# Four moves in a hand-written order: a turn, a fold, a square root and a difference of weights

## The chip, the core and the metric

The kernel runs on one core of a Trainium2 chip. A core has five engines that run side by side, each with its own queue of instructions that is worked off strictly in order: TensorE (PE: matmuls, with its weight loads shown as PEld), VectorE (DVE), ScalarE (ACT), GpSimd (POOL) and SyncE (SP), which here only issues DMAs. Engines wait for one another through semaphores. An instruction that waits holds up everything queued behind it on its engine.

The metric is the device time of one execution in microseconds, as the median of several runs. Times inside an execution come from one profiled execution and are counted from the start of its span.

## What is computed

The input is four batches of 768 tokens, eight heads of 40 features. The first half is an mLSTM cell; the second a Fourier mix with a two-layer network:

```python
for t in range(S):
    m_new = np.maximum(f_gate[:, :, t] + m, i_gate[:, :, t])
    f_stab = np.exp(f_gate[:, :, t] + m - m_new)
    i_stab = np.exp(i_gate[:, :, t] - m_new)
    m = m_new
    C = f_stab * C + i_stab * einsum('bhd,bhe->bhde', vt, kt)
    n = f_stab * n + i_stab * kt
    h_tilde = einsum('bhde,bhe->bhd', C, qt)
    denom = np.maximum(np.abs(nq), 1.0)          # nq = n . q
    y[:, :, t] = sigmoid(o_gate) * h_tilde / denom
x = y as (B, S, H*D)                              # 4 x 768 x 320
u = x + np.real(fft(fft(x, axis=1), axis=2))
un = (u - mean(u)) / np.sqrt(var(u) + 1e-06)      # over the 320 features
out = u + np.maximum(un @ w_ch1, 0.0) @ w_ch2     # 320 -> 1280 -> 320
```

(Indices of the broadcasts are left out.)

## The kernel before

**Stages.** Each batch goes through three stages. The *mLSTM* works on six chunks of 128 tokens; a chunk has scores (L465), an exponential (L421, ACT), a mask (L443, POOL), a weighing (L471, DVE), a product with the state `ph` (L479) and with the chunk (L486), a product into the new state `pc` (L496), a gather (L511 to L529), a *turn*, which is four transposes into a tile `px` (L535, PE), and a *finish*, which divides by the denominator and writes x (L544 to L550, five DVE instructions). The *mix* folds pairs of chunks, (2,3), then (1,4), then (0,5), into even and odd parts (`mix_fold`: L606, L609, L613, L618, L613 on DVE, for pair (2,3) three more on POOL). It multiplies them with tables of cosines and sines, adds the result to x and gets the mean and variance of each row. For batches 2 and 3 `mix_fold_again` folds the folds once more in three steps (POOL L635; DVE L638 with POOL L639 to L642; DVE L644 with POOL L645). The *MLP* of a batch takes 32 slots.

**The order is written by hand.** `at(slot, phase, function, ...)` puts a function into a plan, and `run` calls all of them sorted by slot and, within a slot, by phase: EVAC is 0, FILL 1, MAIN 2, FILL_PE 3, with fractions between. The order of these calls is the order in every engine's queue. MAIN holds the MLP's matmuls, one piece to a slot; everything else is put around them. Batch 0's MLP runs in slots 31 to 62, batch 1's in 63 to 94, batch 2's in 95 to 126, batch 3's in 127 to 158. The mLSTM of batch 1 begins at slot 32 (chunk c at 32 + 3c), of batch 2 at 50, of batch 3 at 82, so each runs beside the MLP of the batch before.

**The sets.** From batch 1 on, the first layer's 10 blocks of 128 hidden features are done as five *sets* of four slots each (`mlp_block`, steps 0 to 3), in a form with seven products in place of eight for two blocks and two groups of tokens. It adds results with DVE: step 1 has one addition (L906, `h12 += p5`), step 2 three (`h12 += p3`, `h22 += p5`, `h11 += p2`), just behind the two tails (L902, matmuls of the remaining 64 features, which add into p3, p5, p2 and p1). Four PSUM banks are used in turn, and in the other direction in every second set. Step 3 begins the next set (L897, in `begin`) in the bank that p3 held, which the first of the three additions frees. A tail into p5 also has to wait for step 1's addition, which reads p5. Set i of batch b occupies the slots s_mlp + 4i to s_mlp + 4i + 3 and i counts from 0, so the third set of batch 1 has its step 1 in slot 72 and its step 2 in 73.

**The second layer** (`mlp_out_pair`, L1016) is in a similar form, for which DVE forms differences of w_ch2 once (`out_weight_sums`, L988, four of them, the last in place). `mix_rstd` computes 1/sqrt(var + 1e-6) for a batch: four DVE operations on 128x6 (L785 to L790), then twelve on POOL (L792 to L795). Its result is first used in the residuals of the second layer (L966).

**The turned chunks' buffers.** `ps_h` is a PSUM pool of two buffers, taken in turn by `ph`, `pc` and, for batches 1 to 3, `px`, in the order of the calls. A new tile waits until the tile before it in the same buffer has been read for the last time: `ph` by the gather's copies on ACT (L517, L519, L524, L528), `pc` by the gather's additions on DVE (L515), `px` by the finish. In batch 1, chunk 2 is turned in slot 45 and finished in 46, chunk 3 turned in 46 and finished in 47, chunk 4 gets its `ph` and `pc` in 47 and is turned in 49, and chunk 5 gets its `ph` in 50.

**Weight pieces.** The weights arrive as float64 and are converted in pieces by DVE and ACT (`take` L344 and L346, `convert` L351 and L352, `join` L358, L360 and L364). The last piece is taken in slot 45 and joined in slot 47.

`plan_mlstm`, `plan_mix` and `plan_batch` fill the plan with these slots. The list that `plan_batch` calls `done` is the slots of the three folds (`x_done` in `plan_mix`): for batch 1 they are 48, 51 and 54.

Of the kernel before, what the change touches and what calls it, by code (L numbers as in the profile page):

```python
# [20 lines left out]
NT = S // L  # L21
# [5 lines left out]
NFF = DFF // L  # L27
TAIL = DM - 2 * L
TG = NT // 2
# [21 lines left out]
def kernel(  # L51
# [70 lines left out]
    def at(slot, phase, fn, *args):  # L122
        plan.setdefault((slot, phase), []).append((fn, args))
# [7 lines left out]
    EVAC, FILL, MAIN, FILL_PE = range(4)  # L131
# [421 lines left out]
    def plan_mlstm(b, s0, stride=3):  # L553
        for c in range(NT):
            s = s0 + stride * c
            if b > 0:
                t = 22 + 2 * c if b == 1 and c < 3 else s - 5
                at(t, FILL, mlstm_load, b, c)
                at(t, FILL, mlstm_load_max, b, c)
                at(t, FILL, mlstm_load_decay, b, c)  # L560
                at(s, FILL, mlstm_load_o, b, c)
            if (b, c) > (0, 0):
                at(s, FILL, mlstm_exp, b, c, 0)
                at(s + 1, FILL - 0.5, mlstm_exp, b, c, NP)
                last = (b, c) == (0, NT - 1)
                at(s - 1 if last else s, FILL_PE + (2.05 if last else 2), mlstm_scores, b, c)
                if b > 0:
                    at(s + 1, FILL, mlstm_mask, b, c)
            at(s, FILL, mlstm_scale_v, b, c)
            at(s if (b, c) == (0, 2) else s + 1, FILL + 0.1, mlstm_scale_q, b, c)  # L570
            at(s + 2, FILL, mlstm_decay, b, c)
            end = (b, c) == (0, NT - 1)
            at(s + 1 if end else s + 2, FILL - 0.4 if end else FILL, mlstm_weigh, b, c)
            at(s + 2 if end else s + 3, FILL_PE, mlstm_from_state, b, c)
            at(s + 2 if end else s + 3, FILL_PE + (2 if end else 3), mlstm_from_chunk, b, c)
            at(s + 3, FILL_PE + 3, mlstm_to_state, b, c)
            at(s + 3 if end else s + 4, FILL, mlstm_gather, b, c)
            if b == 0:
                t, x = ((8, 11), (11, 14), (13, 14), (14, 15.5), (17, 18), (18, 21))[c]
            else:  # L580
                t = s + (8, 8, 7, 5, 5, 5)[c]
                x = t + 1
            at(t, FILL_PE + ((2.5 if c < 4 else 1) if b == 0 else 1), mlstm_turn, b, c, b == 0 and c < 4)
            at(x, FILL + 0.05, mlstm_finish, b, c)
# [212 lines left out]
    def plan_mix(b, s0, x_done, s_feat, s_add, s_turn):  # L797
        for j in range(TG):
            p = TG - 1 - j
            at(x_done[j], FILL + 0.5 if b < 2 else FILL_PE + 0.2, mix_fold, b, p)  # L800
            if b == 0:
                at((s0 - 4, s0 - 2, s0)[j], FILL_PE + 4, mix_seq, b, p, (0, 1))
                at((s0 - 2, s0 - 2, s0)[j], FILL_PE + 4, mix_tail, b, p)
            elif b == 1 or j == 0:
                if b > 1:
                    for step, slot in enumerate((x_done[0], x_done[-1] + 2, x_done[-1] + 6)):
                        at(slot, FILL_PE + 0.25, mix_fold_again, b, step)
                at(s0, FILL_PE + 4, mix_seq, b, p, (0,))
                at(s0 + 1, FILL_PE + 4, mix_seq, b, p, (1,))
                at(s0 + 2, FILL_PE + 4, mix_tail, b, p)  # L810
        for i in range(2):
            at(s0 + 1 if b == 0 else s0 + 1 + i, FILL, mix_seq_out, b, i)
        at(s0 + (1 if b == 0 else 3), FILL + 0.1, mix_tail_out, b)
        for p in range(TG):
            at(s_feat[p], FILL_PE + 4, mix_feat, b, p)
        for c, a, t in zip(ORDER, s_add, s_turn):
            at(a, FILL if b < 2 else MAIN + 0.5, mix_add, b, c)
            at(t, FILL + 0.1, mix_center, b, c)
            at(t, FILL_PE + (5 if b == 0 or c in ORDER[:4] else -0.1), mix_turn, b, c)
            if b > 0:  # L820
                at(t, FILL_PE + 6, mix_turn_out, b, c)
            elif t < s_mlp:
                at(t + 1, FILL + 0.2, mix_turn_out, b, c)
            else:
                at(t + 1, EVAC, mix_turn_out, b, c)
# [221 lines left out]
    def plan_mlp(b, s):  # L1047
        groups = range(NT // TG)
        for i in range(NFF // 2) if b > 0 else ():
            for step in range(4):  # L1050
                at(s, MAIN, mlp_block, b, i, step)
                s += 1
            end = i == NFF // 2 - 1
            for n, (gr, f) in enumerate(((1, 2 * i + 1), (1, 2 * i), (0, 2 * i))):
                at(*((s - 1, MAIN + (-0.1 if gr else 0.1)) if end else (s + n, MAIN + 0.5)), mlp_relu_in_place, gr, f)
        for gr in groups if b == 0 else ():
            for f in range(NFF):
                at(s, MAIN, mlp_in, b, gr, f)
                s += 1
                if f % 2:  # L1060
                    at(s, EVAC, mlp_relu, b, gr, f - 1)
                    at(s, EVAC, mlp_relu, b, gr, f)
        if b > 0:
            for j in range(1, 5):
                at(s - (5, 4, 3, 3)[j - 1], FILL_PE + 0.3, hidden_sums, 0, (j,), 0, NFF // 2 - 2)
            at(s, EVAC, hidden_sums, 0, (1, 2), NFF // 2 - 2, NFF // 2)
            at(s, MAIN + 0.1, hidden_sums, 0, (3, 4), NFF // 2 - 2, NFF // 2)
        for n in range(TG) if b > 0 else ():
            for step in range(4):
                at(s, MAIN, mlp_out_pair, b, n, step)  # L1070
                if n < TG - 1 and step > 1:
                    for j in (2 * step - 3, 2 * step - 2):
                        at(s, MAIN + 0.6, hidden_sums, n + 1, (j,))
                s += 1
        for gr in groups if b == 0 else ():
            for i in range(TG):
                for half in range(2):
                    at(s, MAIN, mlp_out, b, gr, i, half)
                    s += 1
                at(s, EVAC, mlp_store, b, gr, i)  # L1080
# [5 lines left out]

    def plan_batch(b, s_mlstm, s_mix, s_mlp):
        plan_mlstm(b, s_mlstm)
        done = [s_mlstm + 3 * (j + NT // 2) + 7 for j in range(NT // 2)]
        assert s_mix >= done[-1] and s_mlp >= s_mix + 9  # L1090
        late = [s_mlp + 2 * c for c in range(TG)]
        if b == 0:
            feat = [s_mix + 1, s_mix + 1, s_mlp + 3]
            turn = [s_mix + 2, s_mix + 3, s_mix + 4]
            add = turn + [s_mlp, s_mlp + 4, s_mlp + 6]
            late = [s_mlp + 2, s_mlp + 5, s_mlp + 7]
        else:
            feat = [s_mix + c for c in ((3, 4, 6) if b == 1 else (3, 4, 7))]
            add = [s_mix + c for c in ((4, 4, 5, 6, 7, 7) if b == 1 else (4, 4, 5, 6, 8, 9))]
            turn = [s_mix + c for c in ((5, 6, 6) if b == 1 else (6, 7, 8))]  # L1100
            late = [s_mix + c for c in ((7, 8, 8) if b == 1 else (9, 10, 10))]
            at(s_mlp, EVAC + 0.5, mlp_sums)
        plan_mix(b, s_mix, done, feat, add, turn + late)
        at(s_mlp + NFF, FILL + 0.6, mix_rstd, b)
        plan_mlp(b, s_mlp)

    s_mlp = 31
    plan_batch(0, 0, 22, s_mlp)
    plan_batch(1, 32, 54, s_mlp + MLP_SLOTS)
    plan_batch(2, 50, 83, s_mlp + 2 * MLP_SLOTS)  # L1110
    plan_batch(3, 82, 115, s_mlp + 3 * MLP_SLOTS)
    for n in range(4):
        at(s_mlp + 2 * NFF + 1 + n, FILL + 0.4, weight_sums, n)
        at((56, 57, 58, 72)[n], FILL + 0.4, out_weight_sums, n)

    at(60, FILL + 0.4, lambda: nc.gpsimd.memset(ds_sb[0:1, 0, 0, :], 1.0))

# [131 lines left out]
```

## Time and profile before

| | us |
|---|---|
| median of 5 runs | 422.54 |
| the five runs | 422.41, 422.47, 422.54, 423.66, 423.70 |
| the profiled execution's own time | 423.66 |
| its span in the profile | 421.9 |

| engine | busy us | share of the span | instructions |
|---|---|---|---|
| PE | 408.0 | 97% | 2966 |
| PE weight loads | 304.6 | 72% | 2966 |
| DVE | 288.5 | 68% | 682 |
| ACT | 189.0 | 45% | 493 |
| POOL | 112.9 | 27% | 194 |

The span is the time from the first to the last instruction in the profile; the execution's own time has 1.76 us more around it. A busy share is an average over the whole span. Matmuls are pipelined and their ends are modelled, so the busy time of PE says that work is in it, not that it runs at its peak. The granted TensorE clock was 1.00 throughout. The chain of work that ended last consists of PE for 74% of the span, DVE 11%, DMA 8%, issue 3%, ACT 2% and POOL 2%; the DMA pieces of it all lie before 110 us.

### The profile page before, as it was taken

The numbers are of one execution on the slowest core, as the hardware profiler recorded it, in microseconds if no ns is written. First come the engines' busy times: TensorE is split into PE (matmuls) and PEld (weight loads), VectorE is DVE, ScalarE is ACT, GpSimd is POOL, SyncE is SP. The second block draws the span as 40 slices with busy tenths as digits, with TensorE's granted clock in tenths as the row PEclk, the third lists the DMA queues.
The fourth block names the chain that finished last, engine by engine and source line by source line (L and its number), as shares of the span: only waits on it lengthen the run. The fifth ranks groups of instructions, "written<-read, shape, count | busy, mean of one in ns | idle before, by whom it ended". The sixth has DMA issues, their size and how long they took to land.

```text
span 421.9 us, 8013 instructions
## 1 busy us (share of the span) xinstructions
PE 408.0 (97%) x2966; PEld 304.6 (72%) x2966; DVE 288.5 (68%) x682; ACT 189.0 (45%) x493; POOL 112.9 (27%) x194
## 2 busy tenths in 40 slices
PE   8999999999899999999899999999999999999997
PEld 6877554576567678777458899977559989555996
DVE  7789893867895729686855488796844686335552
ACT  6986375677452321664357413554452023355000
POOL 5654201459340720433041341333130000020000
PEclk9999999999999999999999999999999999999999
DMA  7799297457765353364300344310000000000010
GB/s 230 251 270 312 81 274 261 141 181 222 234 161 167 102 154 99 103 207 138 109 0 2 128 125 144 121 54 2 0 2 0 33 31 18 16 2 0 16 48 31
DMA packets 20549, 47.14 MB, mean 112 GB/s; under 512 B 2784, under 2 KB 9312, under 8 KB 20384
## 3 DMA queue, kind: packets, MB, share of 16 engines
q1 hardware_dynamic: 20512, 46.65, 36.3%
q8 instruction: 23, 0.38, 0.4%
q14 instruction: 14, 0.11, 0.1%
HBM read 42.52 MB, written 4.11 MB: 111 GB/s over the span
## 4 chain that ended last, share of the span: by engine, by line
PE 74%; DVE 11%; DMA 8%; issue 3%; ACT 2%; POOL 2%; DVEq 0%; ACTq 0%; POOLq 0%; SPq 0%
PE po L1016 18%; PE pm L897 15%; PE po L960 8%; PE ps L465 5%; PE pm L902 4%; PE ph L486 4%; DMA kvt<-in_kv 4%; PE ph L479 3%; DMA raw<-in_w 3%; PE pu L729 3%; PE px L535 2%; DMA qk<-in_qkT 2%; PE pz L698 2%; PE put L772 1%; PE pM L218 1%
## 5 line engine op out<-in xcount | busy, mean ns | idle before, releaser
L966 DVE SCALAR_TENSOR_TENSOR x<-po,rstd,x 128x160 f32<-128x160 f32 (+1 forms) x69 | 27.0, 395 | 41.4 <-PE po L1016 35.5
L906 DVE TENSOR_TENSOR h<-h,pm 128x384 f32<-128x384 f32 x60 | 30.5, 550 | 31.3 <-PE pm L897 16.0
L421 ACT ACTIVATE W<-W,colT 128x128 f32<-128x128 f32 x144 | 45.0, 395 | 0.0
L443 POOL TENSOR_SCALAR_AFFINE_SELECT W<-W 128x1024 f32<-128x1024 f32 x18 | 21.3, 1184 | 80.2 <-ACT W L421 58.5
L897 PE MATMUL pm<-uT,w_sb 128*128 128x384 f32 x90 | 37.5, 503 | 1.9 <-DVE h L906 1.6
L960 PE MATMUL po<-w_sb,h 128*128 128x320 f32 x120 | 34.4, 435 | 0.0
L471 DVE TENSOR_TENSOR W<-ps,W 128x512 f32<-128x512 f32 x48 | 30.7, 681 | 4.2 <-POOL W L443 4.0
L837 PE MATMUL pm<-uT,w_sb 128*128 128x384 f32 x80 | 29.9, 500 | 1.7 <-DMA qk<-in_qkT 1.0
L777 ACT COPY uT<-put 128x384 f32<-128x384 f32 x24 | 11.2, 478 | 40.2 <-PE put L772 40.2
L960 PEld LDWEIGHTS po<-w_sb,h 128*128 128x128 f32 x120 | 22.2, 190 | 9.5 <-issue 0.8
L1016 PE MATMUL po<-T,S 128*128 128x160 f32 x180 | 27.9, 302 | 0.3 <-DVE x L966 0.3
L465 PE MATMUL ps<-qk 40*128 40x128 f32 x384 | 27.8, 284 | 0.0
L1016 PEld LDWEIGHTS po<-T,S 128*128 128x128 f32 x180 | 25.5, 190 | 1.7 <-DVE x L966 0.5
L792 POOL TENSOR_TENSOR t<-rstd 128x6 f32<-128x6 f32 x12 | 2.9, 244 | 88.5 <-DVE v L790 87.9
L897 PEld LDWEIGHTS pm<-uT,w_sb 128*128 128x128 f32 x90 | 15.5, 189 | 15.4 <-DVE h L906 7.7
L1016 PE MATMUL po<-w_sb,h 128*128 128x160 f32 x180 | 26.5, 301 | 0.0
L465 PEld LDWEIGHTS ps<-qk 40*128 40x128 f32 x384 | 23.4, 187 | 4.1 <-issue 0.7
L1016 PEld LDWEIGHTS po<-w_sb,h 128*128 128x128 f32 x180 | 25.1, 190 | 1.3 <-DVE x L966 0.3
L486 PE MATMUL ph<-W,kvt 128*41 128x128 f32 x384 | 25.8, 277 | 0.0
L524 ACT COPY h<-ph 41x512 f32<-41x512 f32 (+1 forms) x16 | 9.3, 582 | 35.7 <-PE ph L486 35.5
L479 PEld LDWEIGHTS ph<-qg,C 128*128 128x128 f32 x160 | 19.9, 191 | 7.3 <-issue 3.8
L431 POOL TENSOR_TENSOR qg<-qk,Gb 128x512 f32<-128x512 f32 x18 | 25.0, 1388 | 0.1
(207 smaller groups left out, 867.2 us busy)
## 6 DMA issues: line engine op xcount, KB each, us to landing
W<-M_d SPq DMA_DIRECT2D x18, 512.0 KB
kvt<-in_kv SPq DMA_DIRECT2D x24, 324.0 KB
qk<-in_qkT SPq DMA_DIRECT2D x48, 160.0 KB
raw<-in_w SPq DMA_DIRECT2D x10, 640.0 KB
Gb<-G_d SPq DMA_DIRECT2D x36, 128.0 KB
so<-in_o SPq DMA_DIRECT2D x24, 160.0 KB
out<-x SPq DMA_DIRECT2D x24, 160.0 KB
ds_sb<-in_dft_s SPq DMA_DIRECT2D x1, 1155.0 KB
```

What stands on the lines that cost most here:

```text
L421: nc.scalar.activation(out=k.W[:, h, :], in_=M, func=AF.Exp, scale=-1.0, bias=colT[:, c, 0, b * H + h:b * H + h + 1])
L431: nc.gpsimd.tensor_tensor(out=k.qg, in0=k.qk[:, 0], in1=k.Gb, op=OP.mult)
L465: nc.tensor.matmul(k.ps[hip][:, p, :], k.qk[r, 1, p, :], k.qk[r, 0, p, :], start=True, stop=True)
L471: nc.vector.tensor_tensor(out=Wv, in0=k.ps[hip], in1=Wv, op=OP.mult)
L479: nc.tensor.matmul(k.ph[:, p, :], k.C[:, p, :], k.qg[:, p, :], start=(p == 0), stop=False, skip_group_check=True)
L486: nc.tensor.matmul(k.ph[hip * 64:hip * 64 + D1, p, :], k.v1[:, 2 * p + hip, :], k.W[:, 2 * p + hip, :], start=(c == 0 and p == 0), stop=Tr ...
L837: nc.tensor.matmul(k.pm[i], w1_sb[:, ch, f0:f0 + L], u[2 * ch], start=(ch == 0), stop=False)
L897: nc.tensor.matmul(bank, w, u, start=start, stop=True, skip_group_check=True)
L906: nc.vector.tensor_tensor(out=h, in0=h, in1=bank, op=OP.add)
L960: nc.tensor.matmul(k.po, hidden(gr, f)[:, i * L:(i + 1) * L], w2_sb[:, f, :], start=(f == 0), stop=(f == NFF - 1))
L966: nc.vector.scalar_tensor_tensor(out=u, in0=po, scalar=k.rstd[:, c:c + 1], in1=u, op0=OP.mult, op1=OP.add)
L1016: nc.tensor.matmul(po, a[:, f], w[:, f], start=start and f == 0, stop=f == half - 1, skip_group_check=True)
```

## The change

Four calls get another slot; no instruction is added, removed or resized, and no DMA is moved.

- In batch 1, chunk 3 is turned in slot 48 and finished in 49 (before: 46 and 47). The fold of its pair (2,3) moves with it, from slot 48 to 49.
- In batches 2 and 3 the last fold, of pair (0,5), moves by one slot, from 72 to 73 and from 104 to 105. That is beside the third set of the batch before; with the phase FILL_PE + 0.2 it stood behind step 1's addition and stands now behind step 2's three.
- `mix_rstd` of batches 1, 2 and 3 moves by two slots, from 73, 105 and 137 to 75, 107 and 139, with the phase FILL + 0.6, ahead of that slot's MLP step.
- The last `out_weight_sums` (L988, in place on w_ch2) moves from slot 72 to 75, with the phase FILL + 0.4.

```diff
@@ plan_mlstm
-                t = s + (8, 8, 7, 5, 5, 5)[c]
+                t = s + (8, 8, 7, 7 if b == 1 else 5, 5, 5)[c]
                 x = t + 1
             at(t, FILL_PE + ((2.5 if c < 4 else 1) if b == 0 else 1), mlstm_turn, b, c, b == 0 and c < 4)
             at(x, FILL + 0.05, mlstm_finish, b, c)
@@ plan_mix
-            at(x_done[j], FILL + 0.5 if b < 2 else FILL_PE + 0.2, mix_fold, b, p)
+            at(x_done[j] + (b > 1 and j == TG - 1), FILL + 0.5 if b < 2 else FILL_PE + 0.2, mix_fold, b, p)
@@ plan_batch
-        done = [s_mlstm + 3 * (j + NT // 2) + 7 for j in range(NT // 2)]
+        done = [s_mlstm + 3 * (j + NT // 2) + 7 + (b == 1 and j == 0) for j in range(NT // 2)]
...
-        at(s_mlp + NFF, FILL + 0.6, mix_rstd, b)
+        at(s_mlp + NFF + (2 if b > 0 else 0), FILL + 0.6, mix_rstd, b)
@@ the plan
-        at((56, 57, 58, 72)[n], FILL + 0.4, out_weight_sums, n)
+        at((56, 57, 58, 75)[n], FILL + 0.4, out_weight_sums, n)
```

On VectorE the order around the third set of batch 1 is, before: difference of weights (slot 72), one addition, fold, rstd (73), three additions, `mix_fold_again` L638 (74). After: one addition (72), three additions, fold (73), L638 (74), difference of weights, rstd (75), and then the fourth set's one addition (76).

## The prediction

> **What bounds the kernel now.** I read the page's busy shares first: PE is busy 408.0 us of a span of 421.9 at a granted clock of 1.00, so time can be won only in the 13.9 us in which PE stands still. The view of waits, for PE, says who ends these:
>
> ```profile
> PE pm L897 <- DVE h L906: 1.6, 2, 1.1
> PE ph L479 <- DVE den L544: 1.4, 1, 1.4
> ```
>
> The columns are the sum in us, the number of waits, and the longest. Asked by windows, the 1.4 falls at 110 to 125 us, and the 1.6 are one of 1.1 at 200 to 225 and one of 0.5 at 300 to 325. From 110 us on PE has no other wait above 0.4, and from 125 to 200 none at all. So a microsecond taken out of one of the three should reach the end, as long as no other engine becomes late. The change touches the work just ahead of each. The timeline shows each place.
>
> **First place: transposes of the fourth chunk, batch 1.** Start, length, engine, line:
>
> ```profile
> 109.62 1.29 DVE L471 TENSOR_TENSOR W<-ps,W 128x512 f32<-128x512 f32 x2
> ...
> 111.98 0.49 DVE L550 TENSOR_TENSOR x<-px,so 128x320 f32<-128x320 f32 x1
> 112.39 0.15 DVE L544 TENSOR_SCALAR den<-px 128x8 f32<-128x8 f32 x1
> ...
> 112.61 0.35 PE L479 MATMUL ph<-qg,C 128*128 128x128 f32 x1 [1.38 <-DVE den L544]
> ```
>
> PE's L479 (slot 47, `ph` of chunk 4) stands 1.38 us. The view names L544, but the event that fits is the end of the L550 ahead of it, at 112.47: that is the last read of chunk 2's `px`. Pool `ps_h` has two buffers, taken in the order px2, px3, ph4, pc4, so ph4 gets px2's. VectorE is late because its queue stood until 108.69 for a weight piece (L344 after DMA `raw`) and then ran L344, L346, the weighing L471 and chunk 2's finish.
>
> With px3 moved behind ph4 and pc4 the order is px2, ph4, pc4, px3, px4, ph5. Now ph4 takes pc3's buffer, last read by two L515 that end at 107.64, and pc4 takes px2's. PE, step by step: without the four transposes (0.5 us between 108.64 and 109.14) the six L837 start at 108.64 and ph4 comes at 110.7. The scores behind it (+1.05, 111.75) need the `ps` that L471 frees at 110.91; L486 (112.8) needs W, weighed at the same time; pc4 (113.7) needs px2, free at 112.47. None waits. The transposes still cost their 0.5 us, two slots later, so PE's own work is unchanged and 1.38 us are won.
>
> What is late next is chunk 3's finish. It moves from slot 47 to 49, and ph5 now takes px3's buffer. VectorE from 112.4: join of the last weight piece (L358, L360, L364; in this trace 114.02 to 118.31, so 4.3), L515 0.67, L471 1.29, finish 1.65: over at 120.3. PE: pc4 113.7, L837/L841 of slot 48, transposes 115.85, slot 49 to 118.35, px4, slot 50, so ph5 at 120.4 (it was 121.83). It just fits. Here a rule speaks against the change: the Trainium skill, "SBUF — State Buffer", section "Who interferes with whom", has a VectorE instruction with two SBUF inputs and a GpSimd one that reads SBUF exclude each other for a whole instruction. The join has two such inputs; beside the mask and the query product (L443, L431) its L358 and L360 took 1.63 and 1.89 here, where L358's median is 0.82. Alone, the join would take some 2.5 and the finish end at 118.5, with no wait; with every piece at its slowest row (1.88, 1.89, 1.77) it takes 5.5 and ph5 waits 1.2. The join now begins 1.6 earlier, before the mask at 113.88, so I stay by the traced sum and book 0.1 for ph5, with 0 and 1.2 as ends. Sum here: 1.38 - 0.1 = **1.3**.
>
> The fold of pair (2,3) goes along, slot 48 to 49: five VectorE instructions, 1.7 us (118.94 to 120.6), now behind L471 and the finish; and three on POOL (L622 0.52, L609 0.18, L613 0.51), about 1.5 later. POOL was idle 3.15 ahead of them and then 2.18 for ACT ahead of the mask at 124.02, which covers that. VectorE stands 2.11 us before 130.70 for PE's L960: with PE 1.3 earlier that cover shrinks to 0.8 but holds. No DMA is moved, so SP's queue keeps its order.
>
> **Second place: slots 72 and 73, batch 1.**
>
> ```profile
> 206.21 0.98 DVE L988 TENSOR_TENSOR w_sb<-w_sb 128x800 f32<-128x800 f32 x1
> 207.11 0.55 DVE L906 TENSOR_TENSOR h<-h,pm 128x384 f32<-128x384 f32 x1
> ...
> 207.42 1.85 PE L902 MATMUL pm<-uT,w1t_sb 64*128 64x384 f32 x8
> ...
> 207.58 0.48 DVE L606 TENSOR_TENSOR eo<-x 128x320 f32<-128x320 f32 x1
> ...
> 209.72 1.48 DVE L906 TENSOR_TENSOR h<-h,pm 128x384 f32<-128x384 f32 x3
> ...
> 210.32 0.91 PE L897 MATMUL pm<-uT,w_sb 128*128 128x384 f32 x2 [1.06 <-DVE h L906]
> ```
>
> Between the single L906 and the three, VectorE runs the fold (207.58 to 209.17, 1.59) and rstd's four small operations (to 209.72, 0.55); PE's next set needs the bank that the first of the three frees. An undisturbed set (the next one) has its single L906 3.60 after the set's start, L902 at 4.72, the three at 5.66 and the next start at 6.27, that is 1.55 after L902. So PE should resume at 207.42 + 1.55 = 208.97 instead of 210.32: 1.35. That is more than the 1.06 shown, since L902 itself took 1.85 for 1.56: its second tail waits for the single L906, which L988 held up.
>
> After the change VectorE has, from the three L906 (208.36 to 209.75): fold 1.59, L638 0.50, L988 0.90, rstd 0.55, over at 213.3. The next single L906 is due at 208.97 + 3.60 = 212.57, so it is 0.74 late and ends at 213.87, and L902's second tail, due at 213.71, waits until 213.93: **0.2 given back**. L988 now has POOL's L639 to L642 beside it. By the rule above, L988 stands right behind L638 and issues before the first of these, so POOL waits; if POOL were first, L639 (0.31) would push everything and the loss would be 0.5. I take 0.2. rstd's POOL chain (209.82 to 213.48 now) moves behind L642, to about 217.6; its first reader, the residual of this batch, comes after 224.8. Sum: 1.35 - 0.2 = **1.1**.
>
> **Third place: slots 104 and 105, batch 2.**
>
> ```profile
> 302.25 1.56 PE L902 MATMUL pm<-uT,w1t_sb 64*128 64x384 f32 x8
> ...
> 304.36 0.91 PE L897 MATMUL pm<-uT,w_sb 128*128 128x384 f32 x2 [0.55 <-DVE h L906]
> ```
>
> There is no L988 here. 302.25 + 1.55 = 303.80 instead of 304.36: **0.55**. Given back: three L906 to 304.58, fold 306.17, L638 306.67, rstd 307.22; the next single L906 is due at 307.40, so nothing, with 0.18 to spare. In batch 3 rstd moves from one VectorE gap (before L906 at 375.60) into another (377.08 to 379.80): nothing, and its readers come after 389.6.
>
> **The sum.** 1.3 + 1.1 + 0.55 = 2.95 us. The profiled execution took 423.66 (span 421.9 and 1.76 around it), so 420.7 for one like it. The five runs before are 422.41, 422.47, 422.54, 423.66, 423.70: two clusters 1.2 apart, the profiled one in the upper. The median lies in the lower one: 422.54 - 2.95 = **419.6**, if the lower runs have the same three stalls.
>
> **Rivals.** (a) *The lower runs lack the first stall.* The chain of waits into 112.61 goes back through VectorE to a DMA of `raw` (102.25 to 108.59), and a landing can differ from run to run; 1.2 of 1.38 would be gone where it lands early. Then the median has 0.2 + 1.65 to win: 420.7. For it: the sizes match. Against it: the clusters are within 0.13 of themselves, and a shift at the start would look the same. (b) *Chunk 3's finish takes the first gain back* (ph5 waits 1.2, slow join): 422.54 - 1.85 = 420.7. For it the margin of 0.1; against it that the join starts beside an idle POOL. (c) *Slower*: the same VectorE queue ahead of ph5, far longer. PE's lead there is 1.4 and the other two places bring 1.65, so it decides only once the finish ends 3.1 after 120.4, later than 123.5; a finish at 124.5 would give 423.6. Nothing in the trace lengthens a stretch of 7.9 us to 12; even the join's slowest rows give 9.1. (d) *It does nothing here*: if ph4's wait were for chunk 3's own `px` or for W, its move would still leave it, and if PE were held elsewhere the rest would be hidden: 422.5. The windows without any wait of PE speak against it.
>
> **How the numbers follow.** Forecast 0.57 (own range 419.0 to 420.1), (a) 0.17, (b) 0.13, more won than counted 0.05, (d) 0.04, (c) 0.04. Range 418.9 to 421.2 takes in (a) and (b). About 0.2% (0.85 us) is what can be told from no change; (a) and (b) lie beyond it. Faster 0.92, same 0.04, slower 0.04.
>
> **What would show it.** Right: no PE wait at L479 near 111; PE's longest `pm L897 <- DVE h L906` gone at both places; a single L906 of batch 1's fourth set about 0.7 late and its L902 some 0.2 longer; PE's busy time near 408 and a span near 419. Wrong: a wait of PE at ph5 of more than 0.5 (then b); an untouched wait at ph4 (then d); a new wait of PE between 125 and 200.

## The result

| | median us | runs | lowest to highest |
|---|---|---|---|
| before | 421.91 | 18 | 421.17 to 423.7 |
| after | 419.37 | 10 | 418.37 to 420.1 |

The ratio is 0.9935, with a 95% interval of 0.992 to 0.995: 2.7 us less of some 422 (2.1 to 3.4); the two medians differ by 2.54. 2.95 us to 419.6 had been forecast. The two clusters of the first five runs of before don't hold: 15 of the 18 lie between 421.2 and 422.5 and three at 423.7, and the runs of before beside the experiments fill the range from 420.6 to 424.0.

The profiled execution after took 419.37 (span 417.7). The view of waits for PE has neither of the two lines that were shown of before; what is left is led by these:

```profile
PE put L772 <- ACT uc L765: 1.3, 4, 0.4
PE pi L137 <- DVE rest L156: 1.3, 1, 1.3
PE ph L479 <- POOL eo L618: 0.8, 1, 0.8
```

None of them is at the places of the change. The timeline at the first place, where chunk 4 gets its `ph`, and on to chunk 5's:

```profile
107.91 1.29 DVE L471 TENSOR_TENSOR W<-ps,W 128x512 f32<-128x512 f32 x2
109.46 1.05 PE L479 MATMUL ph<-qg,C 128*128 128x128 f32 x8
...
110.28 0.49 DVE L550 TENSOR_TENSOR x<-px,so 128x320 f32<-128x320 f32 x1
...
110.68 0.81 DVE L358 SCALAR_TENSOR_TENSOR e<-raw,e 128x640 uint32<-128x640 uint32 x1
111.42 0.82 DVE L360 SCALAR_TENSOR_TENSOR m<-raw,m 128x640 f32<-128x640 uint32 x1
...
112.27 1.68 DVE L364 TENSOR_TENSOR w_sb<-m,e 128x640 f32<-128x640 f32 x1
...
116.93 0.49 DVE L550 TENSOR_TENSOR x<-px,so 128x320 f32<-128x320 f32 x1
...
118.99 1.16 PE L479 MATMUL ph<-qg,C 128*128 128x128 f32 x8
```

PE's first L479 (109.46) now starts 1.3 us ahead of the end of chunk 2's finish (L550 at 110.28), where before it started just behind it (112.61, end at 112.47). Chunk 3's finish ends at 117.42, and the L479 that depends on it comes 1.57 later.

At the second place, batch 1's third and fourth set:

```profile
204.59 1.56 PE L902 MATMUL pm<-uT,w1t_sb 64*128 64x384 f32 x8
...
205.53 1.49 DVE L906 TENSOR_TENSOR h<-h,pm 128x384 f32<-128x384 f32 x3 [1.51 <-PE pm L902]
206.14 0.91 PE L897 MATMUL pm<-uT,w_sb 128*128 128x384 f32 x2
...
208.71 0.56 DVE L638 TENSOR_TENSOR eo<-fe 128x384 f32<-128x384 f32 x1
...
209.19 0.98 DVE L988 TENSOR_TENSOR w_sb<-w_sb 128x800 f32<-128x800 f32 x1
209.34 1.01 POOL L639 COPY eo<-fe_odd 1x161 f32<-1x161 f32 x1 [15.41 <-DVE eo L638]
...
210.09 0.29 DVE L785 TENSOR_SCALAR v<-x 128x6 f32<-128x6 f32 x1
...
210.77 0.54 DVE L906 TENSOR_TENSOR h<-h,pm 128x384 f32<-128x384 f32 x1
...
210.85 2.07 PE L902 MATMUL pm<-uT,w1t_sb 64*128 64x384 f32 x8
```

PE's L897 follows L902 after 1.55 without a wait. In the fourth set the single L906 ends behind the start of L902, which takes 2.07 in place of 1.56: this is the time given back.

The profiled executions differ by 4.29 us, and their timelines say where. By chunk 2's turn, ahead of anything that was changed, after was already 1.22 earlier (L535 at 105.40, before 106.62); that is a difference between two executions, 0.57 of it there by 67 us. Another 0.73 comes from one more wait for a weight piece, which the change leaves alone (0.08 went again on the way). It is this one of before:

```profile
69.56 0.49 DVE L344 TENSOR_SCALAR e<-raw 128x640 uint32<-128x640 uint32 x1 [6.27 <-DMA raw<-in_w]
...
71.45 0.85 ACT L850 ACTIVATE h<-pm 128x384 f32<-128x384 f32 x2
...
71.97 0.91 PE L837 MATMUL pm<-uT,w_sb 128*128 128x384 f32 x2 [1.00 <-DMA qk<-in_qkT]
```

ScalarE converts the piece (L351, L352) ahead of L850, which reads the bank that this L837 needs. L837 starts 2.41 after L344 here and in after, where the piece came earlier and PE stood only 0.27; the view names L850 there, and a DMA of `qk` here. Six of the twelve profiles have this wait, from 0.24 to 1.00 and always with that 2.41 (2.42 in one); in the six without it L344 came earlier in PE's work. So landings of weight pieces move the time at a second place too, and the change cures one of the two.

From chunk 2's turn to ph5 (121.83 before, 118.99 after) 1.62 were won; from there to batch 1's fourth set 1.34 (its start 210.32, now 206.14, so 4.18 in all); 0.44 were given back in it; 0.55 were won in batch 2 (304.36, now 300.07). 1.22 + 1.62 + 1.34 - 0.44 + 0.55 = 4.29. What was won from chunk 2's turn on is 3.07 in this pair of executions. The 1.62 at the first place are 0.24 more than the wait of 1.38; these lie in steps of 0.1 and less between neighbouring groups of matmuls, and were not followed further.

### The profile page after: what moved, and what is told of

It reads as the page before. It is cut to its first block, busy times and chain, and to the rows that moved or that the text cites. A ratio compares the mean times of both kernels' runs of the same rounds, so it can differ in the third digit from the quotient of the medians.

```text
span 417.7 us, 8020 instructions
## 1 busy us (share of the span) xinstructions
PE 407.2 (98%) x2966; PEld 304.2 (73%) x2966; DVE 288.0 (69%) x682; ACT 189.0 (45%) x493; POOL 114.4 (27%) x194
## 4 chain that ended last, share of the span: by engine, by line
PE 77%; DVE 12%; issue 3%; DMA 3%; ACT 2%; POOL 2%; DVEq 0%; ACTq 0%; POOLq 0%
PE po L1016 18%; PE pm L897 17%; PE po L960 8%; PE pm L902 6%; PE ph L486 4%; PE ps L465 4%; PE ph L479 3%; DMA raw<-in_w 3%; PE pu L729 3%; PE pm L837 2%; PE px L535 2%; PE pz L698 2%; PE pz L686 1%; PE put L772 1%; DVE stats L756 1%
## 5 line engine op out<-in xcount | busy, mean ns | idle before, releaser
L906 DVE TENSOR_TENSOR h<-h,pm 128x384 f32<-128x384 f32 x60 | 30.6, 550 | 29.6 <-PE pm L902 16.6
L897 PE MATMUL pm<-uT,w_sb 128*128 128x384 f32 x90 | 37.5, 504 | 0.2 <-DVE uT L885 0.2
L837 PE MATMUL pm<-uT,w_sb 128*128 128x384 f32 x80 | 29.9, 500 | 0.9 <-DVE x L749 0.5
L897 PEld LDWEIGHTS pm<-uT,w_sb 128*128 128x128 f32 x90 | 15.5, 189 | 13.7 <-DVE h L906 6.0
L902 PE MATMUL pm<-uT,w1t_sb 64*128 64x384 f32 x120 | 24.3, 509 | 0.0
L479 PEld LDWEIGHTS ph<-qg,C 128*128 128x128 f32 x160 | 20.0, 191 | 5.7 <-issue 1.3
```

The source lines that it names most:

```text
L479: nc.tensor.matmul(k.ph[:, p, :], k.C[:, p, :], k.qg[:, p, :], start=(p == 0), stop=False, skip_group_check=True)
L837: nc.tensor.matmul(k.pm[i], w1_sb[:, ch, f0:f0 + L], u[2 * ch], start=(ch == 0), stop=False)
L897: nc.tensor.matmul(bank, w, u, start=start, stop=True, skip_group_check=True)
L902: nc.tensor.matmul(bank, block(w1t_sb, i)[rows], mlp_u(gr, 1)[rows], start=False, stop=True, skip_group_check=True)
L906: nc.vector.tensor_tensor(out=h, in0=h, in1=bank, op=OP.add)
```

## The experiments

Two numbers are read from each profile: the wait of PE at ph4, and the length of batch 1's third and fourth and batch 2's third set, from start to start. A set that waits for nothing takes 6.27 us; the third has four transposes in it and takes 6.71. Starts are counted back from L902, which is 4.71 into a set, and 5.16 into the third; read from L897 to L897 they are the same to 0.02.

| kernel | ratio to before (95%) | wait at ph4 | batch 1, 3rd | 4th | batch 2, 3rd |
|---|---|---|---|---|---|
| before | | 1.38 | 8.06 | 6.27 | 7.26 |
| before again | 1.0002 (0.999 to 1.0014) | 1.16 | 8.06 | 6.27 | 7.26 |
| after | 0.9935 (0.992 to 0.995) | none | 6.71 | 6.71 | 6.71 |
| turn only | 0.9976 (0.9967 to 0.9986) | none | 8.06 | 6.27 | 7.26 |
| all but the turn | 0.9952 (0.9936 to 0.9968) | 0.90 | 6.72 | 6.71 | 6.71 |
| folds only | 0.9961 (0.9949 to 0.9973) | 0.64 | 6.94 | 6.27 | 6.71 |
| rstd and weights only | 0.9964 (0.9951 to 0.9978) | 1.47 | 6.72 | 6.27 | 6.71 |
| last piece taken later | 0.9974 (0.9964 to 0.9984) | none | 8.06 | 6.27 | 7.26 |
| after, weights early | 0.9938 (0.9915 to 0.9962) | none | 6.72 | 6.27 | 6.71 |
| turn, rstd and weights | 0.9926 (0.9909 to 0.9944) | none | 6.72 | 6.27 | 6.71 |

**The turn only.** The edit is the change's first and third hunk (chunk 3's turn and the fold of its pair), nothing else.

> Only the turn of batch 1's chunk 3 (slots 48 and 49, with the fold of its pair). Theory (ph4 waited for chunk 2's px, held by a VectorE queue that a weight piece delays): no wait of PE at ph4 near 110 us, ph5 waits at most 0.2, and 1.3 to 1.6 us less than before, about 420.4; the two sets keep their waits (8.06 us from start to start of batch 1's third set, 7.26 in batch 2). Rival (a) of the prediction, the wait exists only in the slower executions: only 0.2 less, about 421.7. Rival (b), ph5 takes it back: a wait of about 1.2 at ph5 and no gain.

No wait at ph4, none at ph5 (the finish ends 1.57 ahead of it), the sets as before. The time fell by 1.0 us (0.6 to 1.4), less than the 1.3 to 1.6 expected, though the interval reaches into that. Rival (a), 0.2 for most executions, is out, and so is (b).

**All but the turn.** The other hunks.

> Folds, rstd and difference of weights as in the change, chunk 3 turned as before. Theory: the wait at ph4 stays at about 1.4; batch 1's third set 6.71 us from start to start and its fourth 6.71 (0.44 given back), batch 2's 6.71 and 6.27; 1.46 us less than before, about 420.5. Rival (a): this profile shows a wait of some 0.2 at ph4 where the weight piece lands early, and the whole gain of the change (about 2.5) is here.

The set lengths are as expected. The time fell by 2.0 us (1.35 to 2.7), more than the 1.46 that the sets account for, but the interval holds it. The wait at ph4 was 0.90 in this execution, not 1.4. Rival (a) would have a wait of some 0.2 here and a gain of 2.5: the interval alone would allow that gain, but the wait is far longer than 0.2.

**The folds only.**

```diff
-            at(x_done[j], FILL + 0.5 if b < 2 else FILL_PE + 0.2, mix_fold, b, p)
+            at(x_done[j] + (b > 1 and j == TG - 1), FILL + 0.5 if b < 2 else FILL_PE + 0.2, mix_fold, b, p)
```

> Only the last folds of batches 2 and 3 move; rstd and the difference of weights stay ahead of the three additions. Theory (the additions need only so much room as the three tails leave: 1.5 us between the single addition and the three): rstd's 0.55 fits beside the tails and costs nothing, the difference of weights still delays the single addition by 0.28; batch 1's third set 7.0 us from start to start and its fourth 6.27, batch 2's third 6.71; 1.6 us less than before, no less than with all three moved. Rival (each of the three moves is needed and adds its own duration): third set of batch 1 about 7.5, of batch 2 about 7.2, a gain of only 0.6.

**rstd and the difference of weights only.**

```diff
-        at(s_mlp + NFF, FILL + 0.6, mix_rstd, b)
+        at(s_mlp + NFF + (2 if b > 0 else 0), FILL + 0.6, mix_rstd, b)
...
-        at((56, 57, 58, 72)[n], FILL + 0.4, out_weight_sums, n)
+        at((56, 57, 58, 75)[n], FILL + 0.4, out_weight_sums, n)
```

> Only rstd and the difference of weights move behind the additions; the folds stay ahead of the three. Theory: the fold's 1.59 just fills the room between the single addition and the three, so batch 1's third set takes 6.8 us from start to start and its fourth 6.27 (no giving back, since the fold isn't behind), batch 2's third 6.72; 1.75 us less than before, more than with all three. Rival (the fold is what holds the additions): third set of batch 1 7.3 or more, of batch 2 7.2, a gain below 0.8.

In both the sets came out as the theory had them, to 0.1 us, and the rivals' 7.2 to 7.5 did not appear. The time fell by 1.6 us (1.1 to 2.2) and by 1.5 (0.9 to 2.1). By the table, batch 1's third and fourth set together take 14.33 before, 13.42 after, 13.21 with the folds only and 12.99 with rstd and weights only. So at this place either half of the change wins more than the whole, and rstd and weights alone win all there is. Between the single addition and the three, VectorE has about 1.5 us that nobody needs, while PE runs the tails. Rstd's 0.55 fits into that room, and so does a fold of 1.59; both together don't. Moving all three behind the additions overfills the gap behind them instead, and 0.44 goes back. This timeline of the run with rstd and weights moved shows the fit:

```profile
205.60 0.55 DVE L906 TENSOR_TENSOR h<-h,pm 128x384 f32<-128x384 f32 x1
...
206.71 1.56 PE L902 MATMUL pm<-uT,w1t_sb 64*128 64x384 f32 x8
...
207.66 1.48 DVE L906 TENSOR_TENSOR h<-h,pm 128x384 f32<-128x384 f32 x3
```

The three L906 start 0.95 after L902, as where nothing is ahead of them (0.94 in after), although the whole fold was run in between.

**Before again.** No edit.

> The kernel before, unchanged, for another profile and more times. Theory (the wait at ph4 ends with a landing of the last weight piece, so its length is a matter of the execution): L344 starts at another time than 108.69 us relative to PE's work, and the wait at ph4 is somewhere between 0.4 and 1.6 us, longer where L344 starts later after px3; the other two waits are 1.06 and 0.55 again to a hundredth. Rival: the wait at ph4 is a constant 1.4.

The wait at ph4 was 1.16, the other two the same to a hundredth. Over the five profiles with the turn in its old place it was 1.38, 1.16, 0.90, 0.64 and 1.47, mean 1.1. It follows when L344 starts, counted from chunk 3's transposes: 0.05 after them, and 0.54, 0.72 and 0.96 before, and 0.14 after. So its length does hang on that landing, but the shortest, 0.64, came with no DMA wait left ahead of L344: what remains is VectorE's own queue. Rival (a) had only 0.2 left there.

**The last piece taken later.** Before, with L344 and L346 of the last piece behind the weighing and chunk 2's finish:

```diff
-    when += [((s, 0.7), (s + 1, 0.7), (s + 2, 0.6)) for s in (33, 36, 39, 42, 45)]
+    when += [((s, 0.7) if s < 45 else (46, 0.65), (s + 1, 0.7), (s + 2, 0.6)) for s in (33, 36, 39, 42, 45)]
```

> The kernel before with one thing moved: the last weight piece is taken (L344, L346) behind the weighing and chunk 2's finish in VectorE's queue, not ahead of them; chunk 3 is turned as before. Theory (these two stood behind a DMA that they don't need): the wait at ph4 goes, without any move of the transposes, and the time falls by 0.9 to 1.3 us to that of the turn alone. Rival (the order of the two PSUM buffers is what holds ph4, whatever VectorE does): a wait of 1 us or more stays at ph4.

```profile
106.60 1.29 DVE L471 TENSOR_TENSOR W<-ps,W 128x512 f32<-128x512 f32 x2
107.55 0.66 PE L535 MATMUL px<-ident,h 128*128 128x128 f32 x4
108.96 0.49 DVE L550 TENSOR_TENSOR x<-px,so 128x320 f32<-128x320 f32 x1
109.37 0.48 DVE L344 TENSOR_SCALAR e<-raw 128x640 uint32<-128x640 uint32 x1
109.98 1.05 PE L479 MATMUL ph<-qg,C 128*128 128x128 f32 x8
```

The transposes (L535) are still ahead of ph4, and yet ph4 doesn't wait, since L550 is over at 109.45. The gain is that of the turn alone (1.1 against 1.0 us). This shows the chain: chunk 2's finish held ph4's buffer, and the weight piece held the finish. The kernel could be cured at either link.

**Turn, rstd and weights, folds left.** The change without its second hunk.

> The change without its last folds: turn, rstd and difference of weights moved, folds of batches 2 and 3 as before. Theory: as in the run of these two alone, batch 1's third set 6.70 us from start to start and its fourth 6.28 (changed kernel 6.71 and 6.71), batch 2's third 6.70, no wait at ph4: 0.4 us less than the changed kernel, about 2.9 less than before. Rival (the folds are needed once PE is 1.5 us earlier): a wait of PE of 0.5 or more comes back at these sets.

The fourth set is back at 6.27, and no wait came in. The median is 418.94; in time alone it can't be told from after, whose interval overlaps, but the profile has the 0.44 us.

**The difference of weights early.** After, with L988 in slot 66:

```diff
-        at((56, 57, 58, 75)[n], FILL + 0.4, out_weight_sums, n)
+        at((56, 57, 58, 66)[n], FILL + 0.4 if n < 3 else EVAC, out_weight_sums, n)
```

> The changed kernel with the difference of weights (L988) not in slot 75 but in slot 66, in a VectorE gap of batch 1's first set; turn, folds and rstd as in the change. Theory (the 0.44 us that the fourth set gives back comes from the length of the queue fold, L638, L988, rstd ahead of its single addition): without L988's 0.9 the queue is over before that addition is due, batch 1's third and fourth sets take 6.71 and 6.27 us from start to start, and 0.4 less than the changed kernel, about 2.9 less than before. Rival (POOL's L639 to L642 beside it, or a wait of L638 for the fold's own writes, hold the addition): the fourth set stays at 6.5 or more.

The fourth set takes 6.27: the queue's length was the cause of what was given back, and neither POOL nor L638 costs PE anything on its own. The single addition is still 0.25 late there (210.10, due at 209.85), but PE does not wait for it. The time, 419.23, agrees with 0.4 less as with none.

**A later finish.** After, with needless memsets of 128x256 in VectorE's queue ahead of chunk 3's finish. They are added work, for the price of the new wait alone.

```diff
+    for n in range(10):
+        at(49, FILL + 0.04, lambda: nc.vector.memset(rest, 0.0))
```

> The changed kernel with ten needless VectorE memsets of 128x256 ahead of chunk 3's finish, some 2.5 to 3 us, to measure what is left between that finish and ph5 (1.57 us in the profile after). They are added work and go into no result. Theory (ph5 now takes px3's buffer): PE waits at ph5 for the added time less 1.57, so about 1.0 to 1.4, and the kernel is slower than the changed one by about as much. Rival (ph5 doesn't depend on the finish, or px4 does first): no wait at ph5, no loss.

With seven in place of ten:

> As the run with ten needless memsets ahead of chunk 3's finish, with seven, so 2.6 us of added VectorE work. Theory 1 (a wait of PE costs its length, and near 2 us it halves the granted clock for some 6 us more): a wait of 0.7 to 1.1 at ph5, the clock stays at 1.00, and the kernel is slower than the changed one by 0.7 to 1.1, about 420.3. Theory 2 (any wait at this place lowers the clock, for instance by where it falls in a window of time): the clock falls again, and the time is 2 us or more above the changed kernel.

The ten took 3.80 us. The timeline at ph5, and then the view by windows (stretch, length, then busy time and count of PE, PEld, DVE, ACT and POOL, then the granted clock, the DMA share and GB/s):

```profile
119.94 0.49 DVE L550 TENSOR_TENSOR x<-px,so 128x320 f32<-128x320 f32 x1
120.58 1.13 PE L479 MATMUL ph<-qg,C 128*128 128x128 f32 x8 [1.93 <-DVE x L550]
```

```profile
118.60:120.60 2.00, 0.07 (x3) 0.05 (x1) 1.78 (x7) 1.92 (x6) 0.00 (x0) 1.00 0.33 105
120.60:122.00 1.40, 1.40 (x12) 1.28 (x14) 1.33 (x5) 0.10 (x1) 0.51 (x1) 0.91 0.01 6
122.00:124.00 2.00, 2.00 (x20) 1.76 (x20) 1.83 (x5) 0.00 (x0) 1.97 (x4) 0.50 0.00 0
124.00:126.00 2.00, 2.00 (x17) 1.51 (x14) 1.96 (x2) 0.37 (x1) 1.12 (x2) 0.50 0.00 0
126.00:128.00 2.00, 2.00 (x5) 1.25 (x4) 1.83 (x6) 2.00 (x8) 0.00 (x0) 0.50 0.59 201
128.00:132.00 4.00, 4.00 (x15) 2.77 (x15) 1.71 (x3) 0.98 (x4) 0.00 (x0) 0.93 0.31 96
```

The wait is where the theory has it, released by L550 of chunk 3. It was 1.93 us long, against the 1.0 to 1.4 expected, since ten memsets took more than the 2.5 to 3 us assumed. But behind it the granted clock is 0.50 for more than six microseconds. The median is 424.29, the ratio to before 1.0057 (1.0036 to 1.0078) where after has 0.9935: some 5 us, so the wait cost its 1.9 and about 3 more. The profile agrees: from ph5 to batch 1's fourth set PE took 90.36 us against 87.15 in after, 3.2 more, without any other wait in between. The mean clock over the span is 0.991 to 0.996 in all six executions. With seven memsets (2.62 us) the wait was 1.61, more than the 0.7 to 1.1 expected, because the weight piece landed late in that execution (L344 1.93 behind chunk 2's transposes, against 1.07 with ten). The mean clock is 1.00 in all seven executions, and the ratio to before is 0.9958 (0.9941 to 0.9975), about 1.0 us above after's: here the wait costs no more than its own length. Theory 1 holds, with the size of the wait missed.

## Why the prediction was right

**The bound and the three places.** Right. PE's waits at exactly these places are gone, nothing downstream of them cost PE time but the fourth set's single addition (0.44), and the sum of the parts in the two profiles is 3.07 against 2.95. With the mean wait of 1.1 at the first place it is 1.1 + 1.35 - 0.44 + 0.55 = 2.56, which is what the medians show. That the time itself came within 0.2 of 419.6 is in part luck: the base of 422.54, from five runs, was 0.63 above the median of 18, and the gain was put some 0.4 above this sum; the two errors partly cancel.

**First place.** The mechanism was right in each link: px2's buffer (the turn alone takes the wait away), L550 rather than the L544 that the view names, and VectorE's queue behind the piece of weights (the piece taken later takes it away too). Two terms were mis-sized. The 1.38 was one execution's; over five it is 1.1 on average, and the turn alone measured 1.0 and not 1.3. And the 0.1 booked for ph5, with 1.2 as its far end, was nothing: the finish was over 1.57 before ph5 in the profile after, and 1.04 before it in the run with the turn, rstd and weights, where the piece landed late. The join that was given 4.3 us took 3.27 (110.68 to 113.95). It ran ahead of the mask, with L358 and L360 at 0.81 and 0.82, and only L364, which started 0.09 behind the mask, met POOL (1.68). The rule of the Trainium skill, "SBUF — State Buffer", section "Who interferes with whom", would have been the better guide than the traced sum: two instructions that start with POOL idle are not slowed.

**Second place.** 1.35 forecast, 1.34 to 1.35 measured. Given back: 0.2 forecast, 0.44 measured. The single addition was not 0.74 but 1.03 late (due at 206.14 + 3.60 = 209.74, started at 210.77). The fold took 1.78 up to L638, not 1.59: L638 reads what the fold's last instruction has just written and started 0.43 after it, where before rstd's first, which does not, had started 0.24 after it. And rstd took 0.68, not 0.55. L639, which the prediction let wait behind L988, did so (1.01 us in place of 0.31), and it was rstd's first instruction that overlapped it in turn (0.29 in place of 0.16). The prediction took it that all three moves belong together; the runs show that rstd and the weights are enough, and that moving the folds as well costs 0.44.

**Third place.** 0.55 forecast and measured; nothing given back.

**Rivals.** (a) fails on two counts: the lower cluster widened with more runs, and the wait was 0.64 or more in each of the five profiles. (b) did not occur, and (d) is out, since the wait at ph4 went with the turn alone. (c), the slower side, had its place right and its price wrong: it put the point where the new wait turns the change into a loss at a finish 3.1 us late, since it counted a wait at its length. A wait of 1.93 us was enough, because the clock falls behind it.

## What to carry to other kernels

In a queue that is worked off in order, look for what an instruction stands behind without needing it: here a finish stood behind a DMA for another part of the kernel, and moving either of the two was worth the same microsecond. Before moving work out of the way of a chain, measure how much room there is on both sides; some of the pieces may fit where they are, and moving all of them fills the next gap. A stall that depends on a landing is to be sized from several executions, not from one.

## What was not expected of the hardware

A wait of PE of 1.93 us, in the midst of dense work, was followed by a granted clock of 0.50 and cost some 3 us beyond itself. From the rows above the low clock lasted an estimated 6.8 us: 6.00 in full, and 0.25 and 0.56 for the rows with 0.91 and 0.93. Waits of 1.61, 1.47 and 1.38 in other profiles were followed by no such drop. All six executions of that kernel had a lowered mean clock. A mean of 0.996 also stands in one execution with the folds only (423.02) and one with the weights early (421.87), each some 2.6 us above the median of its kernel. Neither was profiled, so where the clock fell in them is not known. Where the border lies, and whether it depends on the moment as well as on the length, is open. The Trainium skill, "TensorE: Matmul & The Clock Gate", section "What's actually happening", has the clock halved after an idle window of about 3.4 us; the wait here was little more than half as long, so for gaps like these the measurement decides.
